# A Mixer's first product by seven block products for eight, in two of three pairs of token groups

## The chip, the cores and the metric

The kernel runs on one core of one Trainium2 chip. The metric is device time of that core: the median of the runs before is 882.91 us (three runs, 880.23 to 884.71). Five engines work beside each other, each with its own queue in order: TensorE (PE; PEld is its loading of weights), VectorE (DVE), ScalarE (ACT), GpSimd (POOL) and SyncE (SP), which issues the DMAs.

## The reference, cut to what matters

Pooled attention over 4 batches of 8 heads (1152 keys, pairs of queries averaged to 576, head size 64), then a Mixer block on the 4 x 576 x 512 result:

```python
xt = x.transpose(0, 2, 1)
h = np.maximum(xt @ w_tok1, 0.0) @ w_tok2
u = x + h.transpose(0, 2, 1)
h2 = np.maximum(u @ w_ch1, 0.0) @ w_ch2     # w_ch1 512 x 1536, w_ch2 1536 x 512
return (u + h2).astype(np.float32)
```

The mixer's weights arrive in double precision. The change touches the line of `h2` alone, the channel mixer.

## The kernel before, in words

Every product of fp32 numbers runs as three products of shorter ones: a high part (the number rounded by ScalarE's copy to fp32r) and a low part (the rest, by a subtraction on VectorE or GpSimd); high by high, low by high and high by low are added in PSUM.

Attention runs head by head: two score products per 128 keys (L954), two exponentials on ScalarE (L968, L971), their difference on GpSimd or VectorE (L975), and the product with v (L1002). After every fourth head `token_mix` (L1099, L1117) mixes the tokens of half a batch; its result u stays in SBUF and goes to DRAM as well (MIXED).

The channel mixer (from L1140) has 2304 rows of u, in six groups of 384 (`groups`), and the 1536 hidden columns in twelve blocks of 128 (`NF`). For each block and group there is a first product, `mm3` (L1233): four chunks of the 512 inputs by three terms, 12 matmuls of 384 columns into one PSUM tile "r"; a ReLU that leaves h in two parts (L1239 on ScalarE, L1241 on VectorE); and a second product, `mm4` (L1261): three chunks of 128 rows by three terms, 9 matmuls of 512 columns into accumulators "a" and "o" that stay open over the twelve blocks. Groups 0 and 1 run together while the weights come in, groups 2 to 5 one by one. `load_ch` brings each weight block in, makes fp32 of it in one step on ScalarE and four on VectorE (L475 to L485) and splits it once (L1186, L1187); all parts stay in SBUF. `make_ut` turns u and splits it: by TensorE for groups 0 and 1 (L1206), from DRAM by small DMAs and a VectorE transpose for the others (L1218), then L1220 and L1222. The last block adds u (L1275) and stores.

What sets the order: all steps are listed with what they read and write, and `Plan.run` issues them in the order of a stored table (ORDER, a permutation of the steps). A second table (OTHER) names the steps that go to their other engine, VectorE for GpSimd mostly. Each engine then takes its instructions strictly in that order.

Of the kernel before, what the change touches and what calls it, by code (L numbers as in the profile page):

```python
# [14 lines left out]
F32 = mybir.dt.float32  # L15
# [91 lines left out]
class Due(dict):  # L107
# [16 lines left out]
    "3GKBGnsrTklU`@MN#q-iJcfts48~Yc&FIWtK{Bl>FX-`&WCqB=WbfRUgkBx}G;B-"
    "cWURiSpzom+Njp8Q1j^t8qH)DDb}wfI+}XJmfSLB;>`<w9xylw(9UpUVCG0apNI-Iv{$nVXu<cMrr(z%66JK)zmh-iGS{27cN)rN}9RO%%p6"
    "aD%w~f2^DU!Et73N6}rRB;9L0V_kB$3cv3wQ7u5;KS3^q-360HXJ;M4sq140l1m72*RSAN!WE0LC8<8#-"
    "gX4_#YWRj#MEH(PaTc|LVt!}e1o4Nq7jA9|&bnMb^2N=69)=v4duiBh)l~gIx99ISnsr1&J$08q9{g(9E%D|TS2li11)leMzpuG4Ys}NWAxY"
    "2TXDv0~$TLtV#<V|Sw34(5+8xbTu3vs(Q`mO#s>4x>|LnFai}iR=b~^NU#Fnr2J7kMv_zl4q&C5JL48GU<LlyXVWq&c@ppayA8Cq`l%GR=2{"
    "PA|DfZQ&IJ-lXi$eH_CFVeG}$w${8ah{^KrPFfyU7++PowS(n@9+$xua5#fZq{a|svi*2<aFixKfg?QlP(C9!KzHZx=SX179MdcI2$}eog92"
    "_P}stW*QN4QFvaPy#rc~fa-OvF$vryLc>T_e6Y#)ut!skb)znPjB@zzrX0F{^(AhU_g?qJV;sw9;QSUzc{Vcr}W=m#uOm`3usx^yWRbng`%A"  # L130
    "~~~+PZ!0E;m?C^vw;lectH^vHjqv46weibw+=1W=XH;VN&;S#Y|vZuQ@Y6X`Hb7dQgl@Z<|uH!_n0=zSUJa^>#_khrvaW$*Us*MFhYj+g9q!"
    "79S6d?(%8X<?n60!baBH)Xcc9{-Garw0hmS;g4q2Bw$i&Wpyjj9Q>%bOxW>W&8e*&XI!c_AF}$~wHnE<wAB;0b}m_22J-"
    "vRz7bAK=T?hfC9d#Iv2+_8W!A$eb7Gfc@)C2NYE#aGYGaj8#?h&MM#((V=2!g6(b}s#H4%7!^NJCzsxv2FnL2!qf!ym}K=kr6r1hjjL`V92z"
    "!^fbtm>G{r?$Sk)+CSVUGdp|qigRh#a8-Bj>>3)sP)G#uWk;0x47!U!mW`dB6GtPp8bn$^Gtd!^R~01-#XI`GU)~PL3F*zx}6mwQ<-"
    "G_Ce@$LV4VT+bjW03(ok^4Y?<KB*wv9=oj=l|imb|c4!N}3<@Qd(T<MD*?rFXBU%X!(Q@wlj@J6v`?Xyny_g`$-"
    "8SwG7i~HBOcOA#y*!N78xuWfT;k8{q#IHILMw^EWr4;5lV=qpqF=^aCEK9W^TQC+6k9yeSP=&E*i+uOse!yU--Sl;Cqpu5x^LDA`*xnqzX77"
    "R{VfO3a_LK4i1lacT97(V9IlQ<>><TjUZ1gu{3&EgFHDxyVMeWwd`7S4|>qWcb)xF41zqa4~Dy*;y346Qk(tt-"
    "|)wC@mqcXop$wwPJ2W1^CcRd|k@l)8lKw%;<5Q@JBUF&F@_bKQBsaD$cPq5J&{$Sw6Va24JKlX8rfBm$SyA#q9W}dn+{_eO-LeXf#E6jcEuf"
    "+AyH{!2)>D$KK8J&`PW%;Nv|3)u5b&=wyo^rAg&&n`M+ow5-"
    "8=t>%@Fs6%%=P1<E5VB4)+y)kaj66kr^$(#^VOQft5cOcF#n|XQb1Q{GjQ<2i|Yj&lvVqubcpkE`VG!?9(8Egb;GI0^cNVWdJ4Y^KG(ZZs-"  # L140
    "%Vg4n48(&(reN^52aqXQ$bO9A4J`>*@$aqQo%px1R8{gH!U>V*L{VMrZk!H}+nwos!@nRTd1$cAnAhL~XG}jk&SX2jKEsKGe1GdwY8%N~-"
    "ZZFOSP#W0$QYXxcV%`tim4x{8J*Y&b0`o3gj>%b3_doyJCuo%B0)<xx`$u`6j4jZe>cFHtnQITtA8m4{~Od1qdlVzpw~oHLWJ(EGE~gfh#K$"
    "%22vebdD88%lsrhQ<ox)#@pJ2jrFekpGUlVqVcWH$^k!p2kCYT*xz32OR5AJ}Z8<^2+Q}q^Vyrs3*cyr^D(}jVNcw?kgoA5~M!%wB5Hr*>B6"
    "nl?w~sgcs>sE}dv9>O@ZN5YmZwO4~0;CF%rQ2ahl4@EJIfFZ!w)&4@4bsYTXrdid{^B!Z;}=h6jk>iui#j)fY377=;=Dp8?<QBA&Y#5~oZ=+"
    "yU9e%ueW&aLvBf1vnie;;gtRn~F4om=I*LyT9&)x8-dtJ=S9_l7#tZ}}g?%d8q74BcNnq<=y$TK#17q^+TC@Yrf|OQG-bJ|nYL-"
# [215 lines left out]
def kernel(  # L361
# [1009 lines left out]
```

## Time and profile before

| | |
|---|---|
| profiled execution, its own time | 885.18 us |
| span of its trace | 883.3 us |
| granted TensorE clock, mean | 0.988 |
| TensorE busy | 852.3 us (96%), 5354 matmuls |
| VectorE busy | 646.8 us (73%) |
| ScalarE busy | 539.7 us (61%) |
| GpSimd busy | 456.5 us (52%) |

In the profile's 40 slices of 22 us TensorE is at 8 or 9 tenths but for the first. VectorE is at 7 to 9 tenths from the second slice to some 660 us and at 0 to 5 behind it; ScalarE falls to 4 tenths and less from some 570 us on, and GpSimd, at 7 to 9 tenths up to 530 us, does nothing from 620 us on. Shares are of the whole span: to see what a change in the mixer is worth, one reads the stretch from 570 us on.

### The profile page before, as it was taken

The page shows a single profiled execution, that of the slowest core. Times are in us where ns is not written, and L with a number is a line of the kernel's source. Part 1 is how long each engine was busy: PE and PEld are TensorE (multiplying, and loading weights), DVE is VectorE, ACT ScalarE, POOL GpSimd, SP SyncE. Part 2 cuts the span into 40 slices and gives each one's busy share as a digit, 9 for nine tenths or more (in the row PEclk, how much of TensorE's full clock was granted, in tenths as well). Part 3 has the DMA queues.
Part 4 walks back from the last instruction along what each step waited for, and adds up shares of the span by engine and source line. Part 5 has one row for each costly group of instructions (what it writes and reads, how often), then busy time and mean ns, then how long its engine had stood idle before and what let it go on. Part 6 is the DMA issues. An engine that isn't in the chain of part 4 may idle for free.

```text
span 883.3 us, 15520 instructions
## 1 busy us (share of the span) xinstructions
PE 852.3 (96%) x5354; PEld 788.0 (89%) x5354; DVE 646.8 (73%) x1321; ACT 539.7 (61%) x1079; POOL 456.5 (52%) x363
## 2 busy tenths in 40 slices
PE   8889998999999999999999999999999999999998
PEld 5778898898999899989989999998999999999987
DVE  5796999998998998997999998988885323021112
ACT  4867887798997897888789889844342211111101
POOL 3897998788999899975888775111000000000000
PEclk9989999999999999999999999999999999999999
DMA  8967776687688678788766553265432311000001
GB/s 179 257 121 131 153 135 131 129 157 141 125 159 145 122 155 151 153 148 148 132 116 140 106 132 90 74 170 142 129 119 51 70 36 41 1 36 1 24 1 48
DMA packets 249597, 99.38 MB, mean 113 GB/s; under 512 B 218352, under 2 KB 232816, under 8 KB 249520
## 3 DMA queue, kind: packets, MB, share of 16 engines
q1 hardware_dynamic: 249520, 98.40, 53.9%
q8 instruction: 42, 0.69, 0.3%
q14 instruction: 35, 0.29, 0.1%
HBM read 46.40 MB, written 9.44 MB: 63 GB/s over the span
## 4 chain that ended last, share of the span: by engine, by line
PE 75%; DVE 8%; DMA 6%; ACT 5%; issue 2%; SPq 2%; POOL 2%; DVEq 0%; ACTq 0%; POOLq 0%
PE r L1233 17%; PE o L1002 15%; PE a L1261 13%; PE s L954 12%; PE r L884 7%; PE o L1261 3%; PE r L1099 3%; PE r L1117 3%; DVE mx L886 2%; DMA kk<-kl 2%; DMA qq<-qh 1%; ACT ph L971 1%; ACT pf L968 1%; DVE sum L982 1%; DMA q<-mh 1%
## 5 line engine op out<-in xcount | busy, mean ns | idle before, releaser
L975 POOL TENSOR_TENSOR pl<-pf,ph 128x576 fp32r<-128x576 f32 x247 | 354.9, 1461 | 85.3 <-PE o L1002 25.1
L1002 PE MATMUL o<-ph,vv 128*64 128x288 f32 (+2 forms) x882 | 208.7, 302 | 3.8 <-POOL vv L814 1.5
L968 ACT ACTIVATE pf<-s 128x576 f32<-128x576 f32 x288 | 191.5, 681 | 30.2 <-PE s L954 27.0
L886 DVE TENSOR_REDUCE mx<-r 128x1 f32<-128x384 f32 x384 | 191.5, 547 | 20.1 <-PE r L884 18.4
L971 ACT ACTIVATE ph<-s 128x576 fp32r<-128x576 f32 x288 | 186.6, 658 | 31.8 <-PE s L954 14.6
L954 PE MATMUL s<-qq,kk 128*128 128x288 f32 x574 | 174.4, 312 | 4.5 <-ACT pf L968 2.3
L954 PE MATMUL s<-q,k 65*128 65x288 f32 x576 | 168.9, 301 | 2.0 <-issue 1.1
L1239 ACT ACTIVATE h<-r 128x384 fp32r<-128x384 f32 x72 | 34.6, 491 | 188.1 <-PE r L1233 186.6
L1002 PE MATMUL o<-pl,vv 128*65 128x288 f32 (+1 forms) x576 | 147.5, 301 | 0.4 <-POOL pl L975 0.4
L1241 DVE SCALAR_TENSOR_TENSOR h<-r,h 128x384 fp32r<-128x384 f32 x72 | 39.0, 555 | 140.9 <-ACT h L1239 140.9
L1002 PEld LDWEIGHTS o<-ph,vv 128*64 128x64 f32 (+2 forms) x882 | 129.8, 154 | 10.9 <-DVE ot L1015 2.4
L884 PE MATMUL r<-kk,qq 128*128 128x384 f32 x372 | 127.9, 356 | 9.1 <-DMA kk<-kl 3.9
L1261 PE MATMUL a<-w,h 128*128 128x512 f32 x504 | 131.6, 393 | 0.0
L954 PEld LDWEIGHTS s<-qq,kk 128*128 128x128 f32 x574 | 111.0, 193 | 11.7 <-ACT pf L968 5.5
L954 PEld LDWEIGHTS s<-q,k 65*128 65x128 f32 x576 | 111.2, 193 | 2.5 <-issue 1.2
L1233 PE MATMUL r<-big,w 128*128 128x384 f32 x576 | 111.5, 336 | 0.0
L1261 PEld LDWEIGHTS a<-w,h 128*128 128x128 f32 x504 | 93.6, 188 | 15.3
L1233 PEld LDWEIGHTS r<-big,w 128*128 128x128 f32 x576 | 102.2, 188 | 5.2
L982 DVE TENSOR_REDUCE sum<-pf 128x96 f32<-128x960 f32 x90 | 101.2, 1135 | 0.2
L1002 PEld LDWEIGHTS o<-pl,vv 128*65 128x65 f32 (+1 forms) x576 | 89.8, 164 | 2.7 <-POOL pl L975 0.7
L884 PEld LDWEIGHTS r<-kk,qq 128*128 128x128 f32 x372 | 70.6, 192 | 18.9 <-issue 5.9
L1233 PE MATMUL r<-ut,w 128*128 128x384 f32 x288 | 58.1, 339 | 0.0
(135 smaller groups left out, 1101.0 us busy)
## 6 DMA issues: line engine op xcount, KB each, us to landing
raw<-in_moe_w_ch_dram SPq DMA_DIRECT2D x24, 512.0 KB, 3.6
vn<-in_v_dram SPq DMA_DIRECT2D x32, 288.0 KB, 3.9
kk<-kh SPq DMA_DIRECT2D x32, 288.0 KB, 3.8
qq<-qh SPq DMA_DIRECT2D x64, 144.0 KB, 3.5
kk<-kl SPq DMA_DIRECT2D x32, 288.0 KB, 4.2
k<-kk SPq DMA_DIRECT2D x31, 288.0 KB, 3.4
qn<-in_q_dram SPq DMA_DIRECT2D x104, 72.0 KB, 2.9
kn<-in_k_dram SPq DMA_DIRECT2D x52, 144.0 KB, 4.0
```

Source lines behind the costliest of these rows:

```text
L884: step(PE, mm(SP3), lambda ps=ps, w=w, x=x: te.matmul(at(ps)[:, 0:SP3], w, x, start=True, stop=True), t, read, [ps], [ps])
L886: step(DVE, dve(SP3), lambda ps=ps, m=m: ve.tensor_reduce(m, at(ps)[:, 0:SP3], axis=AX.X, op=ALU.max), t + due["max_of"], [ps], [key])
L954: te.matmul(at(st)[:, i, 0:HF], w[:, c * P:(c + 1) * P], x[:, fq * HF:(fq + 1) * HF], start=(n == 0), stop=(n == len(terms) - 1))
L968: step(ACT, act_ps(2 * HF) + (0 if near else 49), lambda pf=pf, st=st: sc.activation(pf, at(st)[:, :, 0:HF], AF.Exp, scale=ESC), t, [(st, ...
L971: step(ACT, act_ps(2 * HF) + 15, lambda ph=ph, st=st: sc.activation(at(ph), at(st)[:, :, 0:HF], AF.Exp, scale=ESC), t + due["p_hi"], [(st, ...
L975: both(2 * HF, lambda e, pf=pf, ph=ph, pl=pl: e.tensor_sub(at(pl), pf, f(at(ph))), t + due["p_lo"], [("pf", s), ph], [pl], [pl], on=POOL i ...
L982: step(DVE, 65 + 1.06 * (NK + 1) * HF // CUT, lambda fq=fq, cs=cs: ve.tensor_reduce(SUM[:, fq, cs], PF[:, 5 * fq:5 * fq + 5, cs].rearrange ...
L1002: lambda o=o, x=x, w=w, m=m, i=i, c=c, new=new, end=end: te.matmul(at(o)[0:m - w], VV[i2][:, c, w:m], at(x)[:, i], start=new, stop=end),
L1233: te.matmul(at(ps)[:, 0:GT], w[:, c], x[:, c], start=(c == 0 and n == 0), stop=(c == NC4 - 1 and n == 2))
L1239: step(ACT, act_ps(GT), lambda: sc.activation(at(h)[:, 0], at(ps)[:, 0:GT], AF.Relu), t, [ps], [h])
L1241: step(DVE, dve(GT), lambda: ve.scalar_tensor_tensor(out=at(h)[:, 1], in0=at(ps)[:, 0:GT], scalar=0.0, in1=f(at(h))[:, 0], op0=ALU.max, op ...
L1261: te.matmul(at(ps), a[:, x * P:(x + 1) * P], w, start=(fi == 0 and m == 0), stop=(fi == NF - 1 and m == 2))
```

## The change

Groups 2 and 3, and groups 4 and 5, become pairs. With the hidden blocks k and k + 6 and the two halves of the 512 inputs, a pair's first product is a 2 x 2 block product, and `paired` computes it by seven block products and 15 block additions (Winograd's form of Strassen's scheme) in place of eight products. Each is 6 matmuls of 384 columns (two chunks by three terms, L1294). The sums on the side of u (t1 to t4) are made once per pair (`make_pair`), those on the side of the weights (s1 to s4) per pair and block (`pair_weights`), and the products are added on VectorE out of PSUM (L1365; one per block is copied by ScalarE, L1372). ReLU reads the sums from SBUF (L1302, L1304).

Weights now stay in SBUF as fp32 and are split each time they are used (`split`, L1283 and L1284; `split_w4`, L1396 and L1397), so three times instead of once. Groups 0 and 1 keep the eight products (`plain`). The six accumulators of a pair are open together; one of them is a tile "r". The turned blocks go to SBUF by the transposes (L1251). U[0]'s place in SBUF is used for sums, so u is read back from MIXED for the last addition (L1423, L1429). Both tables are new: 7279 steps for 6860.

```diff
 ORDER = (
-    "c-"
...
-OTHER = (214, 434, 435, 436, 437, 438, 445, 447, 621, 768, 769, 771, 772, 822, 934, 1007, 1161,
...
+OTHER = (20, 218, 434, 435, 436, 437, 438, 447, 619, 620, 621, 623, 632, 768, 769, 770, 772, 923,
...
+    BLOCKS = ("b11", "b21", "t2", "t3", "t1", "t4", "b22")
...
+            either(GT, lambda e, c=c, r=r: e.tensor_sub(
+                stage("t1", c), at(r), stage("b11", c)), t, [r, key("b11", c)], [key("t1", c)])
...
+                stage("t3", c), stage("b22", c), at(r)), t, [r, key("b22", c)], [key("t3", c)])
...
+                stage("t2", c), stage("b22", c), stage("t1", c)), t,
...
+                stage("t4", c), stage("b21", c), stage("t2", c)), t,
...
+    def split(buf, src, read, t, get=True):
+        step(ACT, act(WN), lambda: sc.copy(at(buf)[:, 0], src()), t, read, [buf], [buf])
+        either(WN, lambda e: e.tensor_sub(at(buf)[:, 1], src(), f(at(buf))[:, 0]), t, [*read, buf], [buf])
...
+    def product(ps, w, y, keys, opens, closes, t, after=()):
+        for c in range(H2):
+            def part(c=c):
+                (wb, x) = (at(w), y())
+                for n, (u, v_) in enumerate(((0, 0), (1, 0), (0, 1))):
                     te.matmul(
+                        at(ps)[:, 0:GT], wb[:, u, c * P:(c + 1) * P], x[v_][:, c],
+                        start=(opens and c == 0 and n == 0), stop=(closes and c == H2 - 1 and n == 2))
...
+        split(bufs["a11"], lambda: half(k, 0), wk, t)
+        add("s1", "tensor_add", lambda: half(k2, 0), lambda: half(k2, 1), [])
+        add("s2", "tensor_sub", low("s1"), lambda: half(k, 0), [sums["s1"]])
...
+        add("s3", "tensor_sub", lambda: half(k, 0), lambda: half(k2, 0), [])
...
+        add("s4", "tensor_sub", lambda: half(k, 1), low("s2"), [sums["s2"]])
...
+        p1 = times("a11", "b11")
+        step(ACT, act_ps(GT), lambda: sc.copy(at(u1), at(p1)[:, 0:GT]), t, [p1], [u1], [u1])
+        p6 = times("s2", "t2")
+        add(u2, p6, u1, True)
+        p2 = times("a12", "b21")
+        add(u1, p2, u1)
+        close(u1, h11)
+        p7 = times("s3", "t3")
+        add(u3, p7, u2, True)
+        p5 = times("s1", "t1")
+        add(u4, p5, u3, True)
+        close(u4, h22)
+        add(u2, p5, u2)
+        p4 = times("a22", "t4")
+        add(u3, p4, u3)
+        close(u3, h21)
+        p3 = times("s4", "b22")
+        add(u2, p3, u2)
+        close(u2, h12)
...
+    def split_w4(fi, t):
+        w2 = Buf("w2")
+        step(ACT, act(C), lambda: sc.copy(at(w2)[0], W4[fi]), t, [("w", 4, fi), "rest"], [w2], [w2], after=mixed_pe)
+        either(C, lambda e: e.tensor_sub(at(w2)[1], W4[fi], f(at(w2)[0])), t, [("w", 4, fi), w2], [w2])
...
+            step(DMA, 1.2 * wire(4 * P * C), lambda ob=ob, row=row: sy.dma_start(
+                at(ob), MIXED[row:row + P, :]), t - 10, read, [ob], [ob], after=[*mixes, *uts], pieces=P)
...
-                step(DVE, dve(m), lambda ps=ps, ch=ch, ob=ob, cs=cs: ve.tensor_add(
-                    at(ob)[:, cs], at(ps)[:, cs], U[g][:, ch, cs]), t, [ps] + free, [(ob, y)],
-                    [ob] if y == 0 else [])
+                step(DVE, dve(m), lambda ps=ps, ob=ob, cs=cs: ve.tensor_add(
+                    at(ob)[:, cs], at(ps)[:, cs], at(ob)[:, cs]), t, [ps, ob], [(ob, y)])
...
+    for q2 in range(1, NPAIR):
+        make_pair(q2, t - 60, t)
+        for kc in range(NK6):
+            t += 15
+            wb = pair_weights(kc, t - 16)
+            h11, h22, h21, h12 = paired(wb, t)
```

The order table itself tells a reader nothing, its instructions do. TensorE, in the part of the last groups: before, one first product ("r", from the turned u "big" and weights "w") between second products. The three L1233 rows come four times over, with second products between.

```order
L1261 MATMUL a_6957<-w_6916,h_6950 128x512 x2
L1261 MATMUL a_6957<-w_6917,h_6950 128x512
L1233 MATMUL r_78<-big_70,w_6926 128x384
L1233 MATMUL r_78<-big_70,w_6927 128x384
L1233 MATMUL r_78<-big_71,w_6926 128x384
```

Now, in the first pair of seven products (blocks of u in "ut", "big" and "tt", split weights in "wk", "w2h" and "w2l"):

```order
L1294 MATMUL r_77<-ut_6514,wk_6917 128x384 x6
L1411 MATMUL a_6938<-big_71,h_6928 128x512 x3
L1294 MATMUL r_76<-tt_6930,wk_6916 128x384 x6
L1411 MATMUL a_6940<-big_70,h_6923 128x512 x3
L1294 MATMUL r_77<-big_68,w2l 128x384 x6
L1294 MATMUL r_76<-tt_6931,w2h 128x384 x6
L1411 MATMUL a_6938<-big_70,h_6923 128x512 x3
L1411 MATMUL r_78<-big_70,h_6923 128x512 x3
L1294 MATMUL r_77<-ut_6515,wk_6918 128x384 x6
L1294 MATMUL r_76<-big_69,w2h 128x384 x6
L1294 MATMUL r_77<-tt_6929,wk_6913 128x384 x3
```

A product is 6 matmuls, the tile r_78 is an accumulator here, and r_76 and r_77 take turns; at the end r_77 is filled again after one other product.

VectorE in one of the later groups before: low parts of h (L1241), and the turning of u for the next group.

```order
L1241 SCALAR_TENSOR_TENSOR h_6950<-r_78,h_6950 128x384
L1218 STREAM_TRANSPOSE r_77<-t1l 128x384
L1241 SCALAR_TENSOR_TENSOR h_6951<-r_76,h_6951 128x384
L1241 SCALAR_TENSOR_TENSOR h_6953<-r_78,h_6953 128x384
L1241 SCALAR_TENSOR_TENSOR h_6952<-r_76,h_6952 128x384
L1222 TENSOR_TENSOR big_69<-r_77,big_68 128x384
```

Now, beside the products above:

```order
L1365 TENSOR_TENSOR u_63<-r_76,u_63 128x384
L1284 TENSOR_TENSOR w2h<-ws_6920,w2h 128x256
L1284 TENSOR_TENSOR wk_6913<-wf_6510,wk_6913 128x256
L1365 TENSOR_TENSOR t_6933<-r_77,u_63 128x384
L1333 TENSOR_TENSOR ws_6922<-ws_6921,wf_6510 128x256
L1284 TENSOR_TENSOR wk_6918<-wa_6911,wk_6918 128x256
L1304 SCALAR_TENSOR_TENSOR h_6924<-u_63,h_6924 128x384
L1365 TENSOR_TENSOR u_63<-r_77,u_63 128x384
L1365 TENSOR_TENSOR u_63<-r_76,u_63 128x384
```

Between the low parts of h stand additions of products (L1365), low parts of weights (L1284) and sums of weights (L1333). The end of SP's queue, before:

```order
L1280 DMA out_dram<-raw_6511 128x512
L1280 DMA out_dram<-raw_6510 128x512
L1284 DMA out_dram<-raw_6510 64x512
L1280 DMA out_dram<-raw_6511 128x256 x2
L1366 UNCONDITIONAL_BRANCH
```

and now, with the last three loads of u between stores:

```order
L1433 DMA out_dram<-u_63 128x512 x2
L1433 DMA out_dram<-u_63 128x256 x2
L1423 DMA u_63<-mixed 128x512 x3
L1433 DMA out_dram<-u_63 128x512 x2
L1437 DMA out_dram<-u_63 64x512 x2
```

## Rows read from the trace of the kernel before

**Rows 1.** The page: span, and busy us (share of span) xinstructions of each engine.

```profile
span 883.3 us, 15520 instructions
...
PE 852.3 (96%) x5354; PEld 788.0 (89%) x5354; DVE 646.8 (73%) x1321; ACT 539.7 (61%) x1079; POOL 456.5 (52%) x363
```

**Rows 2.** Stretches: length, busy us of PE, PEld, DVE, ACT, POOL; clock; DMA.

```profile
200.00:300.00 100.00, 96.38 (x693) 91.58 (x692) 93.76 (x194) 86.25 (x172) 92.19 (x70) 1.00 0.74 140
300.00:400.00 100.00, 96.50 (x692) 90.22 (x692) 94.64 (x196) 84.23 (x169) 84.21 (x68) 1.00 0.79 148
400.00:500.00 100.00, 97.76 (x711) 93.50 (x710) 91.83 (x191) 83.79 (x165) 75.84 (x58) 1.00 0.69 132
500.00:600.00 100.00, 99.58 (x712) 96.12 (x711) 91.40 (x186) 76.85 (x152) 39.98 (x30) 1.00 0.46 116
570.00:670.00 100.00, 100.00 (x533) 91.52 (x532) 82.96 (x151) 41.79 (x80) 8.17 (x6) 1.00 0.47 131
670.00:770.00 100.00, 100.00 (x504) 90.68 (x503) 28.79 (x53) 15.09 (x32) 0.00 (x0) 1.00 0.19 43
770.00:880.00 110.00, 109.62 (x549) 98.66 (x547) 19.98 (x37) 12.74 (x27) 0.00 (x0) 1.00 0.05 18
```

**Rows 3.** Waits, 570 to 884 us: us in total, times, longest.

```profile
ACT h L1239 <- PE r L1233: 186.6, 57, 10.6
DVE h L1241 <- ACT h L1239: 140.9, 46, 10.1
...
DVE w L1187 <- ACT w L1186: 2.7, 4, 0.7
```

**Rows 4.** The chain that ended last, at 798 us: start, us, what.

```profile
798.23 4.18 PE r L1233 x24
```

**Rows 5.** Timeline of DVE: start, us, line, operation, tiles.

```profile
605.90 1.02 DVE L1222 TENSOR_TENSOR big<-r,big 128x384 fp32r<-128x384 f32 x2
606.84 0.68 DVE L1187 TENSOR_TENSOR w<-v,w 128x512 fp32r<-128x512 f32 x1
...
620.79 0.69 DVE L1187 TENSOR_TENSOR w<-v,w 128x512 fp32r<-128x512 f32 x1
621.40 0.42 DVE L476 TENSOR_SCALAR v<-v 128x512 f32<-128x512 f32 x1
621.85 0.43 DVE L479 TENSOR_SCALAR v<-v 128x512 uint32<-128x512 uint32 x1
```

**Rows 6.** Groups by line and form: busy us, mean ns; idle before, releaser.

```profile
L1239 ACT ACTIVATE h<-r 128x384 fp32r<-128x384 f32 x72 | 34.6, 491 | 188.1 <-PE r L1233 186.6 <-issue 1.5
L1087 POOL TENSOR_TENSOR big<-u,big 128x256 fp32r<-128x256 f32 x26 | 19.1, 742 | 18.4 <-ACT big L1084 18.1
L1127 DVE TENSOR_TENSOR u<-r,u 128x256 f32<-128x256 f32 x32 | 13.0, 413 | 1.8 <-PE r L1117 1.5
L1055 DVE TENSOR_SCALAR den<-den 128x5 f32<-128x5 f32 x15 | 11.5, 769 | 0.3
L1187 POOL TENSOR_TENSOR w<-v,w 128x512 fp32r<-128x512 f32 x6 | 8.2, 1362 | 65.6 <-ACT w L1186 65.6
L1055 DVE TENSOR_SCALAR den<-r 128x5 f32<-128x5 f32 x17 | 2.6, 154 | 0.2 <-PE r L1036 0.2
```

**Rows 7.** Timeline of POOL and DVE at 591.7 us.

```profile
591.66 1.31 POOL L1187 TENSOR_TENSOR w<-v,w 128x512 fp32r<-128x512 f32 x1 [4.10 <-ACT w L1186]
591.86 1.40 DVE L479 TENSOR_SCALAR v<-v 128x512 uint32<-128x512 uint32 x1
```

**Rows 8.** Timeline of the end.

```profile
876.05 3.56 PE L1261 MATMUL a<-w,h 128*128 128x512 f32 x15
...
879.65 0.76 DVE L1275 TENSOR_TENSOR raw<-a,u 128x256 f32<-128x256 f32 x2 [1.35 <-PE a L1261]
880.11 0.82 SPq L1280 DMA_DIRECT2D out_dram<-raw  x2
```

**Rows 9.** DMA issues: count, KB each, median us to landing.

```profile
out_dram<-raw SPq DMA_DIRECT2D x15, 256.0 KB, 2.2
```

More of the change, by code (lines that the diff above doesn't have):

```diff
@@ L124 @@
[L124 to L133, printed above, removed]
@@ L1181, in load_ch @@
         step(DMA, 1.2 * wire(8 * P * C), load, t - 3, ["first"], [raw], [raw], pieces=4 * P)
[L1182 to L1188 removed]
+        room = "rest" if fi else "first"
@@ L1195, in make_ut, with make_pair, stage, key @@
+        uts.extend(plan.steps[n0:])
+    def make_pair(q, t, t2):
+        def stage(blk, c):
+            x = 2 * BLOCKS.index(blk) + c
+            return f(U[1 - x // 12])[:].rearrange("p c x -> p (c x)")[:, (x % 12) * GT:(x % 12 + 1) * GT]
+        def key(blk, c):
+            return ("stage", blk, c)
+        def turned(half, c, i, out, k, get=()):
+            g, n = groups[i]
+            c = c + H2 * half
+            lb, row = Buf("l"), (18 * g + 2 * n * G) * REM
             read = []
-            for ch in chunks:
+            for ch in range(n * G, (n + 1) * G):
@@ new lines, in make_pair @@
+        for n, blk in enumerate(BLOCKS):
+            old = pe0[n // 2] if q == 1 and n < 4 else ()
+            for c in range(H2):
+                done = ("t", blk, c)
+                step(ACT, act(GT), lambda blk=blk, c=c: sc.copy(T[blk][:, 0, c], stage(blk, c)),
+                     t2, [key(blk, c), "rest"], [done], after=old)
+                either(GT, lambda e, blk=blk, c=c: e.tensor_sub(
+                    T[blk][:, 1, c], stage(blk, c), f(T[blk])[:, 0, c]), t2, [key(blk, c), done], [done])
+            t2 += 1.0
@@ new lines, in relu, with plain_weights @@
+    def relu(src, h, read, t, in_psum):
+        step(ACT, (act_ps if in_psum else act)(GT), lambda: sc.activation(at(h)[:, 0], src(), AF.Relu),
+             t, read, [h], [h])
+        step(DVE, dve(GT), lambda: ve.scalar_tensor_tensor(
+            out=at(h)[:, 1], in0=src(), scalar=0.0, in1=f(at(h))[:, 0],
+            op0=ALU.max, op1=ALU.subtract), t, [*read, h], [h], shared=not in_psum)
+    def plain_weights(fi, t):
+        bufs = [Buf("wb" if fi else "wbf") for _ in range(2)]
+        for o, buf in enumerate(bufs):
+            split(buf, lambda o=o: half(fi, o), [("w", 3, fi), "rest" if fi else "first"], t)
+        return bufs
@@ L1265, in mm4 @@
-            step(PE, 3 * mm(C), part, t, [h, ("w", 4, fi)], [ps],
-                 [ps] if fi == 0 else [], last if i < 2 and fi == 0 else ())
-            if fi < NF - 1:
+                        at(ps), a[:, x * P:(x + 1) * P], b_,
+                        start=(opens and m == 0), stop=(closes and m == 2))
+            step(PE, 3 * mm(C), part, t, [h, w], [ps],
+                 [ps] if opens else [], last if i < 2 and opens else ())
+            if not closes:
                 continue
             ch, ob = n * G + x, Buf("ob")
-            free = [("raw", 4, 2 * NF - 1 - y) for y in range(2)]
@@ L1271, in mm4 @@
-            parts = 2 if i == len(groups) - 1 and x == xs[-1] else 1
+            row = (18 * g + 2 * ch) * REM
+            bs = (2 * g + ch // 4,) if ch < 8 else (2 * g, 2 * g + 1)
+            read = [("mixed", b, y, ch // 8) for b in bs for y in range(2)]
+            step(DMA, 1.2 * wire(4 * P * C), lambda ob=ob, row=row: sy.dma_start(
+                at(ob), MIXED[row:row + P, :]), t - 10, read, [ob], [ob], after=[*mixes, *uts], pieces=P)
+            parts = 2 if i == len(groups) - 2 and x == G - 1 else 1
```

495 lines of the change are left out of this document (284 added, 211 removed), and 21 rows, old and new, of the table OTHER.

## The prediction, made before the changed kernel ran

> **What bounds the kernel now.** I read the summary first: TensorE is busy 852.3 of 883.3 us [rows 1], so the kernel is TensorE's. Then I cut the span into stretches [rows 2]. In the attention part (three stretches from 200 to 500 us) VectorE is busy 92 to 95% and GpSimd 76 to 92%, and TensorE idles 2.2 to 3.6 us in each 100. From 570 us on, the channel mixer runs: TensorE idles 0.4 us in 310, its granted clock is 1.00 (2.4 GHz), and VectorE falls from 83% to 29% and then 18%. The waits of that part [rows 3] say the same from the other side: ScalarE waits 186.6 us for the first product's PSUM tile and VectorE 140.9 us for ScalarE. So in the last 300 us each TensorE instruction costs its full issue time, and VectorE and ScalarE have room. That is the stage the change works in.
>
> **What is removed.** Four of the six groups of tokens (two pairs) run their first product in seven block products where there were eight. By the order TensorE has 792 matmuls of 384 columns in the mixer's first product for 864: 72 fewer. A run of 24 of them took 4.18 us on the chain [rows 4], 0.174 us each: 72 x 0.174 = 12.5 us. The second product keeps its 648 matmuls, and attention all of its own. Since TensorE has no idle time there, the whole 12.5 us comes off unless TensorE begins to wait.
>
> **What is added on the other engines.** Durations first. VectorE's starts are closer together than its busy times: two 384-wide subtractions and the next start at 605.90 and 606.84, 0.47 us each; a 512-wide one 0.61 us to the next start; for 256 columns the same slope gives 0.33 us (an estimate from these two) [rows 5].
> - VectorE loses 18 subtractions of 512 (11.0 us) and 16 of 384 (7.5 us). It gains, by the order, 84 additions of products out of PSUM, 26 low parts of blocks and 15 block sums, all 384 wide (125 x 0.47 = 58.8 us), 67 low parts of weights and 26 weight sums of 256 (93 x 0.33 = 30.7 us), and 32 low parts of the second weights of 512 (19.5 us). Net +90.5 us on 131.7 us (the last three stretches of [rows 2] added): 222 us in the 297 us that would be left, 75%.
> - GpSimd gains 63 instructions of 256, 4 of 512 and 3 of 384 for 6 of 512. At 0.742 and 1.362 us [rows 6], and 1.05 between them for 384: about 55 us in all for 8.2 [rows 2].
> - ScalarE gains 144 copies net; at 0.49 us each, the time of a 384-wide one [rows 6], where most are 256 wide: 71 us on 70 (the three last stretches of [rows 2]), under half of the stage. It stays covered.
>
> In total nothing overflows, but it is uneven. The unpacking of the weights (four VectorE steps, 24 times) must be over within the first pair, as before. In that first 100 us the low parts of both weights (24 x 0.33 + 12 x 0.61 = 15.2 us) and the preparation of the first seven-product pair (8 sums and 14 low parts, 10.3 us) come to the 83.0 us that were there, and 11.0 us of old subtractions go: about 97 us of VectorE work for 100 us of TensorE work. That is above the 94.6% at which TensorE idled 3.5 us in 100 [rows 2]. The bounds: 0.4 us per 100 (the stretch from 500 to 600, VectorE 91%) and, nothing in the trace being fuller, twice 3.6. I take 3.5 us for this stretch. For the 197 us of the two pairs VectorE has 125 us and GpSimd some 45.
>
> **The product chain.** A product is six matmuls, 1.05 us. With six accumulators open in a pair, two PSUM tiles are left for the products where there were three, and a tile is free again only after VectorE has read it (0.55 us, behind whatever VectorE has begun). By the order 8 of the 84 products begin with only one other product since their tile was last filled; the other places have matmuls of the second product between as well. At those eight: 0.55 us fits into 1.05; with another instruction of VectorE ahead of it, 0.47 to 0.61 us, it is late by up to 0.1 us plus the signals. Bounds 0 and 0.5 us each; I take 0.2 us, 1.6 us in sum.
>
> **Shared access to SBUF.** A VectorE instruction on 128x5 elements takes 0.154 us when it reads PSUM and 0.769 us when it reads SBUF [rows 6], and while GpSimd ran from 591.66 for 1.31 us a VectorE instruction that takes 0.43 us elsewhere [rows 5] took 1.40 and ended 0.3 us behind it [rows 7]. So VectorE can be held up for a whole GpSimd instruction. The Trainium skill, SBUF — State Buffer, "Who interferes with whom", says that VectorE instructions with two SBUF inputs also exclude GpSimd ones that read SBUF, and that the later one blocks fully. If that holds for all of the added work, the mixer's VectorE and GpSimd times add up to 222 + 55 = 277 of 297 us instead of lying beside each other; the pair of [rows 7] shows it for one-input instructions of the unpacking only. By that rule in full the forecast below would be 881.5 us for 875.9.
>
> By the rows alone I let it cost nothing beyond the stalls above, since the additions out of PSUM are like the 0.154 us case; VectorE and GpSimd taking turns throughout is the second rival.
>
> **Tail and the rest.** Before, the last addition is cut in two; the last matmul's end is 879.61 and the span's 883.3, 3.7 us [rows 8]. Now the last addition is 512 wide (0.69 us, where 0.46 passed from the first half's start to the first store) with two stores behind it: +0.3 us. The last three chunks' residual is loaded into tiles that the stores before must have left: a store lands 2.2 us after its issue [rows 9], a load of the same size I put at the same, 27 matmuls of 0.23 us (6.2 us) stand between, so it just fits; +0.1 us. SP's queue gets 18 loads of the residual's rows, each of which waits until a store has left its tile, 2.2 us at most [rows 9]; behind them stand stores and the next pair's block loads, whose data are wanted more than a product later, so I put 0 for them, and up to 2.2 us where a block load is late once per pair.
>
> Attention: its instructions per engine are the same within a handful, but the order is another everywhere. Of TensorE's 31.0 us of idle [rows 1] 27 lie before 570 us, and per 100 us it varies by about 0.7 around 3.1 [rows 2]; two orders of five such stretches can so differ by 2 to 3 us either way. I put 0.
>
> **Sum**, against the profiled execution (885.18 us, 1.9 us more than its span): 885.2 - 12.5 + 3.5 + 1.6 + 0.4 = 878.2 us. That execution is 2.3 us over the median of the timed runs (882.91), so I forecast 875.9 us, 0.8% less.
>
> **Rivals.**
> 1. Cover nearly complete: VectorE's lead over TensorE absorbs the full stretch, so that 0.4 us per 100, 1.2 us, stand in place of 5.1: 872.0 us, and down to 869 with attention up to 3 us better. For it: TensorE idled only 0.4 us at 91% VectorE. Against: no stretch at 97%.
> 2. Full exclusion: VectorE and GpSimd take turns, 277 of 297 us, 93%, the state of 200 to 400 us, where TensorE idled 3.6 us per 100. Then 10.7 us of stalls replace 5.1: 881.5 us, no difference that can be told (a measurement here tells about 0.5%, 4.4 us). For it: [rows 6, 7]. Against: VectorE's additions read PSUM.
> 3. Slower: VectorE becomes the mixer's bound. Its queue is in order, and each of 197 low parts (weights, blocks and h) waits for ScalarE's high part. If each costs it w us on top of the 277, TensorE's 310 us of before are passed from w = 0.17. The nearest old case, the 128x512 low part, waited 2.7 us in 18 instructions, 0.15 each [rows 3]. At 0.2 us: 277 + 39 = 316 us, 19 us over the 297: about 889 us. Against it: most of those low parts stand some instructions behind their high part in the order, and the full exclusion must hold as well.
>
> That the 72 matmuls are not saved is no rival, since the order shows them gone.
>
> **Chances.** Forecast and its neighbourhood (873.5 to 878.5) 0.42, rival 1 0.24, rival 2 0.19, rival 3 0.15. Faster by more than 0.5% (under 878.5): 0.66; within: 0.19; slower (over 887.3): 0.15. The range from 868.5 to 886 leaves out rival 3 and a little below; the likeliest case alone has 872 to 879.
>
> **What would show it.** Right: 72 matmuls fewer in the first product at 0.174 us; TensorE's idle after 570 us some 3 to 8 us, most of it in the first 100, released by VectorE; VectorE near 95% there and 60 to 75% behind. Wrong: waits of the first product on VectorE of 10 us or more in the two pairs, VectorE's 256-wide instructions with two SBUF inputs much longer than the 0.413 us of one out of PSUM [rows 6] (exclusion), clock rows under 1.00 after 570 us, or an idle before 570 us that differs from 27 us by more than 3.

## The result, and the profile after

The changed kernel takes 861.78 us (median of four runs, 859.35 to 862.09) beside 883.33 us for the kernel before on the same chip: ratio 0.9755, 95% interval 0.9723 to 0.9786, some 21.6 us less. The forecast was 875.9 us and its range ended at 868.5, so the gain was forecast far too small. The profiled execution took 862.01 us for 885.18. Its summary, to be read beside [rows 1]:

```profile
span 860.2 us, 15845 instructions
...
PE 837.7 (97%) x5282; PEld 773.9 (90%) x5282; DVE 736.7 (86%) x1541; ACT 588.5 (68%) x1215; POOL 512.5 (60%) x431
```

TensorE has the 72 matmuls fewer (5282 for 5354) and is busy 14.6 us less; the other 8.5 us are idle time that went. To see where, I cut both spans at the start of the mixer's first product and at the end of the last matmul (first product at 569.74 us before and 557.04 after). Columns as in [rows 2]; first the kernel before, then the changed one:

```profile
0.00:569.74 569.74, 542.45 (x3773) 506.92 (x3773) 514.43 (x1081) 469.94 (x940) 448.29 (x357) 0.98 0.71 140
569.74:879.62 309.88, 309.88 (x1584) 281.11 (x1582) 131.61 (x239) 69.79 (x139) 8.17 (x6) 1.00 0.23 62
```

```profile
0.00:557.04 557.04, 539.49 (x3769) 504.67 (x3770) 506.76 (x1082) 464.14 (x933) 450.66 (x361) 0.98 0.73 143
557.04:855.44 298.40, 298.24 (x1515) 269.22 (x1513) 229.04 (x459) 124.41 (x283) 61.82 (x70) 1.00 0.29 80
```

| part | before | after | difference | forecast |
|---|---|---|---|---|
| attention, up to the first product | 569.74 | 557.04 | -12.7 | 0 |
| channel mixer, to the last matmul | 309.88 | 298.40 | -11.5 | -7.4 |
| tail, to the end of the span | 3.7 | 4.8 | +1.1 | +0.4 |

More than half of the gain lies in attention, whose computation the change leaves alone: its idle time falls from 27.3 us (569.74 less 542.45) to 17.6. The other 3.0 us are shorter busy time. In the mixer TensorE idles 0.16 us of 298.40, and 11.5 of the 12.5 us of the 72 matmuls came off. The same stretches as [rows 2], after:

```profile
200.00:300.00 100.00, 97.94 (x706) 93.35 (x705) 95.32 (x193) 88.41 (x178) 91.30 (x70) 1.00 0.74 140
300.00:400.00 100.00, 99.17 (x718) 94.65 (x717) 94.56 (x204) 85.87 (x173) 80.90 (x66) 1.00 0.82 160
400.00:500.00 100.00, 99.82 (x733) 95.99 (x732) 92.69 (x200) 84.71 (x166) 83.91 (x63) 1.00 0.66 129
560.00:660.00 100.00, 99.84 (x527) 91.15 (x526) 90.04 (x184) 45.65 (x100) 8.86 (x10) 1.00 0.53 144
660.00:760.00 100.00, 100.00 (x499) 90.08 (x498) 78.65 (x157) 46.30 (x110) 30.18 (x34) 1.00 0.18 44
760.00:850.00 90.00, 90.00 (x447) 80.87 (x446) 56.31 (x111) 30.83 (x71) 22.78 (x27) 1.00 0.13 41
```

VectorE is as busy in attention as it was (92.7 to 95.3%), yet TensorE idles 2.1, 0.8 and 0.2 us in these three stretches where it was 3.6, 3.5 and 2.2 [rows 2]. In the mixer's first 100 us VectorE is at 90.0%, not at the 97% of the forecast.

The tail, to be read beside [rows 8], from the timeline, with the last three loads' row of the DMA issues (count, KB each, median us to landing) at its end:

```profile
850.67 1.75 SPq L1423 DMA_DIRECT2D u<-mixed  x3
853.24 2.20 PE L1411 MATMUL r<-big,h 128*128 128x512 f32 x9
854.36 1.29 DVE L1429 TENSOR_TENSOR u<-a,u 128x512 f32<-128x512 f32 x2 [4.24 <-DMA u<-mixed]
855.68 0.69 DVE L1429 TENSOR_TENSOR u<-r,u 128x512 f32<-128x512 f32 x1
856.40 1.11 SPq L1437 DMA_DIRECT2D out_dram<-u  x2
...
u<-mixed SPq DMA_DIRECT2D x3, 256.0 KB, 3.3
```

VectorE waits 4.24 us for the first of the last three loads of u, which was issued at 850.67 us and landed at 853.91. Two additions run late, the third load lands at 855.56, and so the last addition starts 0.24 us behind the last matmul (855.44). It is 0.69 us long, and its two stores take 1.11 us to issue.

### The profile page after: what moved, and what is told of

It is laid out like the page before. It is cut to its first block, busy times and chain, and to the rows that moved or that the text cites. A ratio compares the mean times of both kernels' runs of the same rounds, so it can differ in the third digit from the quotient of the medians.

```text
span 860.2 us, 15845 instructions
## 1 busy us (share of the span) xinstructions
PE 837.7 (97%) x5282; PEld 773.9 (90%) x5282; DVE 736.7 (86%) x1541; ACT 588.5 (68%) x1215; POOL 512.5 (60%) x431
## 4 chain that ended last, share of the span: by engine, by line
PE 81%; DVE 9%; DMA 3%; ACT 2%; issue 2%; SPq 1%; POOL 1%; DVEq 0%; ACTq 0%
PE o L1011 18%; PE r L1294 16%; PE s L963 14%; PE a L1411 11%; PE r L893 8%; PE r L1108 3%; PE o L1411 3%; DVE mx L895 3%; PE r L1411 3%; PE r L1126 2%; DVE sum L991 2%; PE r L1045 1%; ACT pf L977 1%; PE r L1053 1%; SPq L869 1%
## 5 line engine op out<-in xcount | busy, mean ns | idle before, releaser
L1011 PE MATMUL o<-ph,vv 128*65 128x288 f32 (+2 forms) x882 | 211.3, 304 | 2.4 <-DVE ot L1024 1.6
L1011 PEld LDWEIGHTS o<-ph,vv 128*65 128x65 f32 (+2 forms) x882 | 130.8, 155 | 8.0 <-DVE ot L1024 3.1
L893 PE MATMUL r<-kk,qq 128*128 128x384 f32 x372 | 124.2, 354 | 4.1 <-DMA qq<-qh 1.3
L1411 PE MATMUL a<-big,h 128*128 128x512 f32 x432 | 113.0, 392 | 0.0
L1411 PEld LDWEIGHTS a<-big,h 128*128 128x128 f32 x432 | 80.4, 188 | 13.4
L893 PEld LDWEIGHTS r<-kk,qq 128*128 128x128 f32 x372 | 69.9, 191 | 13.2 <-DVE mx L895 6.5
L1284 POOL TENSOR_TENSOR wk<-wa,wk 128x256 fp32r<-128x256 f32 x22 | 18.1, 829 | 78.2 <-ACT wk L1283 78.1
L1294 PE MATMUL r<-ut,wk 128*128 128x384 f32 x276 | 56.8, 339 | 0.1
L1365 DVE TENSOR_TENSOR u<-r,u 128x384 f32<-128x384 f32 x58 | 31.6, 552 | 26.8 <-PE r L1294 26.3
L1294 PEld LDWEIGHTS r<-ut,wk 128*128 128x128 f32 x276 | 49.5, 188 | 2.7 <-DVE big L1224 0.3
L823 POOL TENSOR_TENSOR vv<-vn,vv 128x576 fp32r<-128x576 f32 x26 | 35.3, 1356 | 6.1 <-ACT vv L820 5.9
```

Source lines behind the costliest of these rows:

```text
L823: both(NK * D, lambda e: e.tensor_sub(vv[:, :, lo], vn, f(vv)[:, :, hi]), t, ["vn", ("vv", h % 2)], [("vv", h % 2)])
L893: step(PE, mm(SP3), lambda ps=ps, w=w, x=x: te.matmul(at(ps)[:, 0:SP3], w, x, start=True, stop=True), t, read, [ps], [ps])
L1011: lambda o=o, x=x, w=w, m=m, i=i, c=c, new=new, end=end: te.matmul(at(o)[0:m - w], VV[i2][:, c, w:m], at(x)[:, i], start=new, stop=end),
L1294: te.matmul(at(ps)[:, 0:GT], wb[:, u, c * P:(c + 1) * P], x[v_][:, c], start=(opens and c == 0 and n == 0), stop=(closes and c == H2 - 1 a ...
L1365: step(DVE, dve(GT), lambda: ve.tensor_add(at(out_), at(a)[:, 0:GT], at(b_)), t, [a, b_], [out_], [out_] if get else [])
L1411: te.matmul(at(ps), a[:, x * P:(x + 1) * P], b_, start=(opens and m == 0), stop=(closes and m == 2))
```

## Experiments: attention or mixer

Attention and token mixing are the same 5842 steps in both kernels, so their order and engines can be exchanged.

**First experiment: attention's tables alone.** In the kernel before (the tables are packed, so their edits are told in words here and below):

```diff
 # ORDER, OTHER: steps 0 to 5841
-order among themselves and engines of the kernel before
+order among themselves and engines of the changed kernel
```

> The kernel before, with its eight-product mixer untouched, but the 5842 steps of attention and token mixing in the changed kernel's order and on its engines. Theory 1, the new order alone makes attention shorter (first product of the mixer at 557.0 us for 569.7): about 871 us, 12 to 13 less than before, with TensorE's idle time ahead of the mixer near 17.5 us for 27.3. Rival, attention gains because the new mixer asks less of the engines or of SBUF beside it (other weight unpacking, other tiles), so its order alone gives nothing: 883 us, idle ahead of the mixer near 27 us.

Measured: 874.45 us, ratio 0.9892 (0.9863 to 0.9921), 9.5 us less. **Second experiment: the reverse**, the changed kernel with attention's old tables.

> The changed kernel, with the steps of attention and token mixing in the order and on the engines of the kernel before; the mixer's seven products stay. Theory 1: what is left is the mixer's own gain, 11.5 us, less 1.1 us at the tail: about 873 us. Rival (the gain in attention comes with the new mixer): 862 us, as the changed kernel. The forecast's own size for this part (7.0 us less): 876 us.

Measured: 876.37 us, ratio 0.9919 (0.9897 to 0.9941), 7.2 us less. The stretches of the first and of the second:

```profile
0.00:556.33 556.33, 537.85 (x3769) 501.78 (x3770) 507.96 (x1085) 464.69 (x934) 450.64 (x361) 0.99 0.73 143
556.33:868.23 311.90, 310.62 (x1587) 281.66 (x1585) 132.50 (x239) 69.18 (x138) 8.04 (x6) 1.00 0.23 61
```

```profile
0.00:569.46 569.46, 539.73 (x3772) 502.02 (x3773) 514.98 (x1078) 468.21 (x939) 446.64 (x357) 0.99 0.72 140
569.46:869.47 300.01, 298.78 (x1512) 269.07 (x1510) 229.01 (x459) 124.71 (x284) 61.78 (x70) 1.00 0.29 79
```

With the new tables attention ends at 556 to 557 us whichever mixer follows, with the old ones at 569 to 570. So the tables make the 12.7 us, not the new mixer beside them, and theory 1 holds. Each exchange costs 2.0 and 1.6 us in the mixer (311.90 for 309.88, 300.01 for 298.40), most likely because two parts meet whose orders were not made for each other; that is a good part of the 3 us by which both medians came out above the theory's 871 and 873 us. The clock is not the cause: over all of attention its mean is 0.98 in both kernels (rows above). Its mean over the first and second 100 us was 0.93 and 0.97 in the kernel before and 0.95 and 1.00 in the second experiment, and yet attention, in the same order, ended at the same time.

## Experiments: the price of a matmul, and VectorE's cover

**Third experiment.** In the changed kernel, the product of w11 and u11:

```diff
-                for n, (u, v_) in enumerate(((0, 0), (1, 0), (0, 1))):
+                for c in ((0, 1, 0) if twice and c == 0 else (c,)):
+                    for n, (u, v_) in enumerate(((0, 0), (1, 0), (0, 1))):
...
-                           True, True, t, done)
+                           True, True, t, done, w == "a11")
```

> The changed kernel, in which one of the seven products of each block (that of w11 and u11) runs its six matmuls a second time, so that TensorE has the 72 matmuls of 384 columns again; the other engines' work is the same. Theory: TensorE sets the pace through both pairs, 72 x 0.174 = 12.5 us more, 874.3 us. Rival: VectorE or a product's PSUM tile sets it in places and hides a part; 7 us more or less, up to 869 us.

Measured: 874.72 us, ratio 0.9892 (0.9868 to 0.9916); the mixer takes 311.15 us for 298.40, 12.75 more, 0.177 us for a matmul. **Fourth experiment**, two products of each block at half their depth:

```diff
+                if half_ and c == 1:
+                    return
...
-                           True, True, t, done)
+                           True, True, t, done, w in ("a12", "s1"))
```

> The changed kernel, in which two of the seven products of each block (w12 by u21, and that of s1 and t1) run over 128 of their 256 inputs only, so that TensorE has 72 matmuls fewer still; the other engines' work is the same and the output leaves those terms out. Theory: VectorE, busy 137 us of the last 200, still covers: 12.5 us less, 849.3 us, with under 2 us of new waits. Rival: the chain of products and additions is at its limit already, so less than half comes off: 856 us or more, with TensorE waiting for VectorE's reads of the product tiles.

Measured: 850.25 us, ratio 0.9619 (0.9601 to 0.9637); the mixer takes 288.35 us, 10.05 less where 12.5 were expected (the medians differ by 11.5), with one row of waits on TensorE:

```profile
PE r L1296 <- DVE u L1367: 0.6, 3, 0.2
```

So TensorE sets the mixer's pace, and four fifths or more of another such cut would still come off. Products of half the length begin to wait for VectorE's reading of their tile, but these waits are 0.6 us of the 2.4 us that did not come off; where the rest goes is not shown.

**Eighth experiment**: in the changed kernel the mixer's 70 GpSimd steps go to VectorE.

```diff
 # OTHER
-..., 5810, 6032, 6034, ..., 7197, 7243,)
+..., 5810,)
```

> The changed kernel with the 70 steps that GpSimd does in the channel mixer given to VectorE (some 25 us more there, 252 of the mixer's 298 us). Theory, VectorE's lead covers it and GpSimd does not hold VectorE up: 862 to 864 us. Rival A (my forecast's term: at 95% and more VectorE makes TensorE wait): the first 100 us of the mixer and the pairs get waits on VectorE, 866 us and more. Rival B (the two engines take turns, the second rival of the forecast): nothing is lost or 1 us is won, 860 to 862 us, since VectorE's own instructions get shorter without GpSimd.

Measured: 861.28 us, ratio 0.9720 (0.9691 to 0.9750), no difference from the changed kernel that can be told; the number lies in Rival B's range. VectorE's groups by form, of the changed kernel and then of this one:

```profile
L1365 DVE TENSOR_TENSOR u<-r,u 128x384 f32<-128x384 f32 x58 | 31.6, 552 | 26.8 <-PE r L1294 26.3
L1304 DVE SCALAR_TENSOR_TENSOR h<-u,h 128x384 fp32r<-128x384 f32 x36 | 23.3, 655 | 3.5 <-ACT h L1302 3.4
L1284 DVE TENSOR_TENSOR wk<-wa,wk 128x256 fp32r<-128x256 f32 x32 | 15.0, 470 | 5.6 <-ACT wk L1283 5.6
```

```profile
L1365 DVE TENSOR_TENSOR u<-r,u 128x384 f32<-128x384 f32 x58 | 31.5, 552 | 18.8 <-PE r L1294 18.6
L1304 DVE SCALAR_TENSOR_TENSOR h<-u,h 128x384 fp32r<-128x384 f32 x36 | 19.6, 552 | 2.2 <-ACT h L1302 2.2
L1284 DVE TENSOR_TENSOR wk<-wa,wk 128x256 fp32r<-128x256 f32 x54 | 22.4, 418 | 6.4 <-ACT wk L1283 6.2
```

Additions out of PSUM take 552 ns with or without GpSimd; instructions whose operands all lie in SBUF are 103 and 52 ns longer beside it. VectorE's busy time in the mixer rises by 15.1 us (229.04 to 244.11), though the steps that come over take about 30.7 by their own durations (63 x 0.418, 4 x 0.685 and 3 x 0.55): by this difference the other half, 15.6 us, had been delay by GpSimd. So Rival B's mechanism is there, and the 15.1 us that remain are covered, as the theory has it.

**Eleventh and twelfth experiments**: work is added on VectorE while the weights are unpacked.

```diff
-        either(C, lambda e: e.tensor_sub(at(w2)[1], W4[fi], f(at(w2)[0])), ...
+        either(C, lambda e: [e.tensor_sub(at(w2)[1], W4[fi], f(at(w2)[0])) for _ in range(n)], ...
...
-        w2 = split_w4(fi, t - 4)
+        w2 = split_w4(fi, t - 4, 2)
```

The twelfth doubles the subtraction of `split` for the first weights in the same way.

> The changed kernel, in which the low part of each of the 12 second weights is computed twice in a row on VectorE while the first two groups run (12 x 0.61 = 7.3 us more in a stretch of 100 us in which VectorE is busy 90.0 and TensorE idles 0.16 us). Theory 2, VectorE's lead covers up to its full time: within 1 us of the changed kernel, 862 to 863 us, TensorE's idle in the stretch under 1 us at some 97% VectorE. Rival, my forecast's term (3.5 us of waits at 97%): 865 to 866 us.

> As the eleventh, and 18 of the low parts of the first weights on VectorE (18 x 0.33 = 5.9 us) and 6 on GpSimd twice as well: 13.2 us more on VectorE, 103 us of work in the first 100. Theory 2: TensorE waits for what passes VectorE's full time, 3 to 5 us: 865 to 867 us. Rival, the waits set in earlier and add up: 870 us and more; second rival, VectorE falls behind and makes it up in the pairs, where it has room: 862 to 863 us.

Measured: 864.02 us, ratio 0.9764 (0.9731 to 0.9797), and 874.41 us, ratio 0.9888 (0.9849 to 0.9928). First 100 us and whole mixer, of the eleventh and then of the twelfth:

```profile
560.00:660.00 100.00, 98.42 (x504) 86.70 (x503) 93.19 (x186) 43.72 (x96) 8.95 (x10) 1.00 0.53 141
556.04:858.22 302.18, 300.60 (x1515) 268.40 (x1513) 236.77 (x471) 124.58 (x283) 61.95 (x70) 1.00 0.29 79
```

```profile
560.00:660.00 100.00, 93.39 (x483) 81.12 (x481) 93.52 (x191) 41.20 (x92) 11.66 (x13) 1.00 0.50 134
560.73:871.41 310.68, 302.68 (x1515) 268.16 (x1513) 244.99 (x487) 124.61 (x283) 67.00 (x76) 1.00 0.28 77
```

In the traces the first 7.3 us of extra work make the mixer 3.8 us longer (302.18 for 298.40), 13.2 us make it 12.3 longer. The medians are 2.2 and 12.6 us above the changed kernel's; for the eleventh alone the ratios (0.9764 and 0.9755) tell no difference, so that its 3.8 us rest on one trace. Theory 2 falls with the twelfth: in this stretch the cover ends where VectorE's busy share is between 90 and 93%. The twelfth has more in it than VectorE's load, however: GpSimd's six low parts are doubled as well, 1.6 us of TensorE's waits end with them, and its trace is of an execution of 878.00 us, 3.6 above its median. The rows also warn that TensorE's idle time can understate a loss: 1.6 and 8.0 us are idle, the rest of the 3.8 and 12.3 stands in longer busy time of the same 1515 matmuls.

## Experiments: what in attention's tables gives the gain

All in the kernel before. The **fifth** takes the order alone, the **sixth** the engines alone, the **seventh** the places of the 594 DMA steps alone.

```diff
 # ORDER, OTHER: steps 0 to 5841
-(5) order   (6) engines   (7) places of the DMA steps: of the kernel before
+(5) order   (6) engines   (7) places of the DMA steps: of the changed kernel
```

> The kernel before with attention's steps in the changed kernel's order, but each on the engine that the kernel before gives it (its own table of engines). Theory 1a, the order of issue is what makes attention shorter (first experiment: 9.5 us of its median): 873 to 876 us. Rival 1b, the choice of engine for 92 steps (8 more products with 1/den on VectorE, 4 fewer subtractions there) makes it: 881 to 884 us, no difference.

> The kernel before in its own order; only the engines of attention's steps are those of the changed kernel. Theory 1a: no gain, 881 to 886 us, since the order was made for the other choice. Rival 1b: 874 to 876 us.

> The kernel before, in which only attention's 594 DMA steps stand where the changed kernel's order has them; all other engines keep their order and their work. TensorE's idle time ahead of the mixer that ended with a DMA was 6.9 us before and 1.7 us in the changed kernel. Theory 1c, the earlier issue of these DMAs is worth that much by itself: 878 to 880 us. Rival: TensorE then waits for the next engine instead, 882 to 884 us.

Measured: 889.18 us, ratio 1.0048 (1.0029 to 1.0067); 894.37 us, 1.0094 (1.0061 to 1.0128); 898.42 us, 1.0150 (1.0108 to 1.0192). All three are slower than the kernel before, by 4.2, 8.3 and 13.3 us, while order and engines together are 9.5 us faster: neither is a gain by itself. Theories 1a, 1b and 1c fall. The seventh also has a lower clock, 0.97 over attention for 0.98 before; whether as cause or effect of its delay is not shown:

```profile
0.00:582.30 582.30, 548.17 (x3772) 511.08 (x3773) 515.25 (x1081) 470.68 (x940) 448.25 (x357) 0.97 0.69 137
```

The **ninth**, **tenth**, **thirteenth** and **fourteenth** take order and engines together, for a part of the heads.

```diff
 # ORDER, OTHER: steps of heads
+(9) 0 to 15   (10) 16 to 31   (13) 0 to 23   (14) 0 to 7: as in the changed kernel
```

> The kernel before; of attention's steps only those of the first 16 heads have the changed kernel's order and engines, the other 16 heads and the mixer keep their own. The first experiment's trace was 8.7 us ahead of the trace of before after 7 of 16 parts of the scores and 13.5 us at their end. Theory 1d, the gain is spread over the heads, so each half has its part: 5 to 8 us here, 877 to 880 us on the scale of 885. Rival, the seam between two orders costs as much as the mixed tables of experiments 5 to 7 did: 885 us and more.

> The same the other way round: the last 16 heads' steps in the changed kernel's order and on its engines, the first 16 as before. Theory 1d: 4 to 6 us less, 879 to 881 us; with the ninth experiment some 10 to 12 us in all. Rival, the gain comes from the first heads alone, where TensorE idles most: 884 to 886 us here.

> The kernel before with the changed kernel's order and engines for attention's steps of the first 24 heads. Theory 1e (both orders run at their own pace up to a seam, and the seam between them costs a fixed sum, 6 to 7 us in the ninth experiment): ahead of the seam the trace is 10 to 12 us before that of the kernel before (it was 436 us there at 12 of 16 parts of the scores), then gives 6 to 7 us back: 880 to 881 us on the scale of 885. Rival 1f (the new order is worth nothing unless it is whole): 885 us and more, with the loss spread over the last heads.

> The same for the first 8 heads. Theory 1e: 4 to 6 us ahead before the seam (169 us there in the kernel before at 4 of 16 parts), 6 to 7 us given back: 885 to 888 us. Rival 1f: 885 us and more as well, but without the lead ahead of the seam.

Measured: ratios 1.0000 (0.9983 to 1.0018), 1.0048 (1.0028 to 1.0069), 1.0012 (0.9993 to 1.0031) and 1.0009 (0.9990 to 1.0028). The traces show how. The stretch from the 577th to the 793rd of the 1154 score matmuls (heads 16 to 21, just behind the seam of the ninth), in the kernel before, in the changed one and in the ninth experiment:

```profile
298.08:401.70 103.62, 100.10 (x722) 93.63 (x720) 98.17 (x205) 87.75 (x177) 87.83 (x70) 1.00 0.79 149
```

```profile
291.71:391.58 99.87, 98.87 (x715) 93.97 (x713) 97.02 (x207) 86.52 (x175) 83.31 (x67) 1.00 0.79 152
```

```profile
291.76:402.25 110.49, 103.39 (x720) 94.78 (x719) 102.12 (x211) 87.65 (x176) 84.29 (x67) 0.98 0.75 139
```

The thirteenth from head 22, and the kernel before over the same score matmuls:

```profile
393.43:498.95 105.52, 98.71 (x709) 92.75 (x707) 91.20 (x193) 81.96 (x158) 77.45 (x59) 1.00 0.65 123
```

```profile
401.70:500.70 99.00, 96.76 (x703) 92.50 (x702) 90.92 (x187) 82.71 (x163) 74.84 (x57) 1.00 0.68 130
```

The ninth arrives with the changed kernel's lead (291.76, 6.3 us ahead of 298.08) and leaves with none. So does the fourteenth, with 5.7 us of lead at head 8. The thirteenth has 8.3 us at head 22 and loses 6.5 of them by head 28, at a clock of 1.00 (so the ninth's 0.98 is not what the loss needs), and one more by the end; the tenth, which begins in the old order, gains nothing behind its seam to the end either. In all four attention ends at 568.9 to 569.5 us. The gain is spread over the heads, but behind the seam the lead is lost but for a us or less, whatever its size. That is neither theory 1e (a fixed sum) nor 1f (no lead at all).

**Fifteenth and sixteenth.** Over the 1080 VectorE instructions of attention, what the durations have above the lower quartile of the same form in the kernel before sums to 18.2 us in the kernel before, 21.3 in the second experiment and 9.5 in the changed kernel. The largest part is the addition of a constant to 128x5 sums, 769 ns each in [rows 6]; after:

```profile
L1064 DVE TENSOR_SCALAR den<-den 128x5 f32<-128x5 f32 x15 | 6.3, 421 | 0.3
L1067 DVE RECIPROCAL rd<-den 128x5 f32<-128x5 f32 x32 | 5.8, 182 | 0.5
L1064 DVE TENSOR_SCALAR den<-r 128x5 f32<-128x5 f32 x17 | 2.6, 154 | 2.1 <-PE r L1045 2.1
```

In both kernels the sums were put into PSUM:

```diff
-                den[:, 0:4, 0], at(part).rearrange("p (c x) -> p c x", c=4), axis=AX.X, op=ALU.add),
+                total(0, 4), at(part).rearrange("p (c x) -> p c x", c=4), axis=AX.X, op=ALU.add),
...
-            den, turned()[:, :, D:DT] if pv else den, EPS),
+            den, turned()[:, :, D:DT] if pv else total(0, 5).unsqueeze(2), EPS),
```

> The kernel before, in its own order; the 15 sums of 128x5 numbers to which VectorE adds a constant (0.769 us each where they lie in SBUF, 0.154 where they lie in PSUM) are put into free columns of a PSUM tile by the reduction before them. Nothing else changes. Theory 3, in attention VectorE is delayed by GpSimd on instructions of which all operands lie in SBUF, and this is what the new order avoids (the 15 take 11.5 us in the kernel before, 13.2 in the second experiment's trace, 6.3 in the changed kernel, 5.8 in the first experiment's): 15 x 0.615 = 9.2 us of VectorE's time back, and as VectorE is at 90% and more there, 5 to 9 us of the whole: 876 to 880 us on the scale of 884.5. Rival, the delays fall into time that VectorE has anyway: 883 to 885 us.

> The same edit in the changed kernel, where the 15 take 6.3 us (0.421 each): 15 x 0.267 = 4.0 us of VectorE's time back. Theory 3: 2 to 4 us less than the changed kernel, 858 to 860 us. Rival: no difference, 861.5 to 863 us.

Measured: 882.12 us, ratio 0.9978 (0.9962 to 0.9993), 2 us less in the old order; in the new one 864.24 us, 0.9782 (0.9762 to 0.9802), no gain. The additions fall to 158 ns each, but the reductions now hold the tile in which TensorE turns the next output. TensorE's waits from 100 to 560 us in the sixteenth:

```profile
PE r L1045 <- DVE r L1057: 3.1, 6, 0.7
PE r L893 <- DMA qq<-qh: 1.5, 1, 1.5
```

The collision is real, and avoiding it in this way is worth some 2 us of the old order, not the 12.7; what it would be worth without the new waits on the tile is not shown. Two sums over the traces tell more. VectorE's delay, counted as above, is 12.9 us in the thirteenth, whose attention ends at 568.96 us, and 6.7 in the sixteenth, whose attention ends at 560.56, 3.5 us behind the changed kernel's with 9.5. TensorE's idle time that ended with a DMA is 0.3 us in the fifth, less than the changed kernel's 1.7, and attention ends at 571.64 there. So less of either does not bring the gain by itself. What in the tables makes the 12.7 us stays open: the experiments show that it takes order and engines together, over all heads.

## Why the prediction was wrong, step by step

- **The step that failed: "Attention: ... I put 0", with 2 to 3 us either way.** That spread was taken from differences between stretches of one order, and says nothing of another order. The bound stood in [rows 1]: of 31.0 us of idle time 27.3 lie in attention, which a new order and new engines may take or add to. Measured -12.7, of which 9.7 are idle time; the first two experiments put it on the tables, and what in them does it stays open. It is most of the 16.2 us by which the profiled execution (862.01) lies below the sum (878.2), and it is the prediction's own last sign of being wrong: 17.6 us of idle time there for 27.
- **72 matmuls at 0.174 us: right.** The third experiment has 0.177.
- **VectorE's stalls, 3.5 us at 97%: wrong load, and a price that fits in part by luck.** The stretch was at 90% and lost next to nothing. I had added 10.3 us of preparation of the first pair to it; of its 22 instructions 15 run there on VectorE, two on GpSimd, and five come later. And 42 unpacking steps of 484 and 516 ns before take some 427 now: four of them had taken 1.05 to 1.40 us beside GpSimd's 512-wide steps [rows 7], which are gone from the stretch, some 3 us that I had left in. As to the price, the eleventh experiment, which adds 7.3 us to the measured 90%, makes the mixer 3.8 us longer in its trace. But I had it from attention's 94.6%, and in the new order 94.6% goes with 0.8 us of idle time (300 to 400 us, after) where it was 3.5: a busy share has no price of its own.
- **Product chain, 1.6 us: no idle time.** TensorE idles 0.00 us in the two last stretches, and stalls and chain together cost no more than some 1.0 us, by which the mixer's 11.5 falls short of 12.5 (1.3 at the third experiment's price). The fourth experiment finds the first waits of this kind, 0.6 us, with products of half the length.
- **Shared access, put at 0 beyond the stalls: right in the time.** The delays on VectorE exist (15.6 us by the eighth experiment) and in its rows strike instructions with SBUF operands alone, as the Trainium skill (SBUF — State Buffer, "Who interferes with whom") has it for instructions with two SBUF inputs; with GpSimd busy 61.8 us in the mixer they are far from the full exclusion of the second rival, and they are hidden.
- **Tail, +0.4: +1.1.** The late loads (3.3 us to landing where I took 2.2), and two stores that take 1.11 us to issue where 0.82 stood [rows 8].
- **Rivals.** The first (cover nearly complete, 872 us, 869 with attention 3 us better) had the mixer right; even it allowed attention too little. The second and the third did not come; the twelfth experiment shows that VectorE's room in the first 100 us was small, since 13.2 us more there cost 12.3. Two slips change nothing: the 0.4 us of idle time that I read in the mixer lie behind the last matmul, and the third rival's terms add up to 890 us, not 889.

## What to carry to other kernels

Where a change comes with a new order for the whole program, the unchanged part is not unchanged: its idle time is what the new order can win, and it belongs in the range. Tables made together can't be judged apart: here order, engines and DMA places each lost time alone, and a part of an order lost its lead behind the place where it met the other. For cover, work out the load of the stretch before pricing it: here 0.16 us was idle with VectorE at 90%, 7.3 us more on VectorE cost 2 to 4 us, and 13.2 us more cost 12.

## Not expected of the hardware

Beside GpSimd, VectorE's addition of a constant on 128x5 elements in SBUF takes 421 to 883 ns (mean of the 15 in the changed kernel and in the second experiment) for 154 out of PSUM, while a reciprocal of the same 128x5 in SBUF takes 180 to 183 in every trace, though GpSimd was at work at the start of 24 of its 32 in the kernel before: GpSimd holds up one of these two kinds of instruction and not the other. And a loss can be half hidden in busy rows: in the eleventh experiment 3.8 us of longer mixer show as 1.4 us of idle time more.
